# A gated mix of two attentions: f32r halves in row pairs, one stream of slots, masks inside the row maxima, outputs at unit ends, part of A's queries projected late

## The chip, the cores and the metric

The kernel runs on one core of a Trainium2 chip, in one launch. The core has five engines that run side by side and meet only through semaphores: TensorE (PE, matmuls, with its weight loads shown as PEld), VectorE (DVE), ScalarE (ACT), GpSimd (POOL) and SyncE (SP, which here issues most DMAs). Matmuls write to PSUM, eight banks of 512 f32 numbers on each of 128 partitions. The metric is the device time of one execution in microseconds (us).

## The reference

Everything is float32. `x` is 2048 tokens by 512; both attentions read the same `x` and have 32 heads of 16 dimensions.

```python
g = sigmoid((x * gate_w).sum(-1, keepdims=True))
# A: softmax attention over all 2048 keys, no mask
q, k, v = split(x @ A_wqkv)
a = softmax(q k^T * 0.25) v @ A_wo
# B: four segments of 512 tokens; causal inside a segment, and a memory of the earlier segments
p = softmax(q_s k_s^T * 0.25 + causal_mask) v_s
a_mem = (phi(q_s) @ M) / (phi(q_s) @ z + 1e-6);  phi(t) = t + 1 if t > 0 else exp(t)
o = sigmoid(beta) * a_mem + (1 - sigmoid(beta)) * p
M += phi(k_s)^T v_s;  z += sum phi(k_s)
b = o @ B_wo
out = g * a + (1 - g) * b
```

## The kernel before, in words

The source is one long schedule written out by hand: the order in which the Python code calls an engine is the order in that engine's queue, and each engine stops at the first instruction whose semaphores are not ready. No planner reorders anything.

**Projections** (in the block `p0`, L228 to L494). A *slot* is the twelve products of one 128 x 512 tile of q, k or v: four contraction tiles by three terms, since x and the weights are each split into a rounded f32r half and the rest. There are 96 slots: for A, 4 chunks of 512 tokens times (4 tiles of q, 4 of k, 4 of v); then the same for B with its memory (`mem_q`, `mem_den`, `mem_k`). `qk_tile` splits each tile of q and k into three bf16 parts (L294 to L316) and stores them in DRAM scratch, `qd` and `kd`. From slot 51 on, `some_max` puts the first row maxima beside the products.

**Attention.** Work is cut into *units* (side, group of 4 heads, chunk of 512 queries). A has 32 units of 16 steps, one for each block of 128 keys; B has 32 units of 4 steps. All A units come first, in the order group then chunk, then all B units. One step has for each of its 4 heads: a *maximum*, run ahead of the scores by 22 steps (12 in B), in which PE multiplies 128 queries by 512 keys in 96 rows of bf16 parts (L174, L185) and DVE reduces the bank to a row maximum (L176; in B L190 adds the causal mask on the way and writes the bank again); a *score* (L560), in which PE multiplies 128 keys by up to 512 queries with 99 rows, three of which carry the negated maximum, and ACT takes the exponential (L563); and the *values* (L579), in which P of an earlier step is multiplied in f32 with 17 columns of v (16 dimensions and a one for the row sum), the four heads in four column groups of the array, two instructions each. In B, POOL zeroes the masked triangle of P (L565). When a unit's maxima are done, `finish_max` splits them on POOL into three bf16 parts, `transpose_max` turns them on PE, and a DMA writes them as rows 96 to 98 of the q tile (L157). PSUM in this part: 3 banks for maxima, 3 for scores, 1 for values, 1 for the rest.

K of A is loaded once for a group (four chunks, three DMAs each, L125 to L127) and used by its four units; q once for each unit (L116 to L118). Loads are issued on SP five steps ahead of the maxima.

**Outputs.** `oraw` (L583) goes to DRAM, the row sums come back, are inverted on DVE, multiplied by gates, sent out, and read back spread over the heads' rows; the scaled rows are split into f32r halves and multiplied by `wo` (L721). For A the scaling runs an octet of heads over all tokens at a time; the output products run beside the B steps, a segment behind, and the last segment's after the last step.

The names that the change and the prediction touch: `load_q`, `load_k`, `max_parts`, `finish_max`, `transpose_max`, `some_max`, `qk_tile`, `score_parts`, `values`, the functions from `invert_load` to `out_products`, and the loop over `steps` at the end.

Of the kernel before, what the change touches and what calls it, by code (L numbers as in the profile page):

```python
# [12 lines left out]
BF16 = mybir.dt.bfloat16  # L13
# [6 lines left out]
S = 2048  # L20
# [9 lines left out]
MASKED = -1.0e9 / SCALE  # L30

LEAD_A = 22         # steps by which the row maxima run ahead of the scores
LEAD_B = 12
LAG_A = 2           # steps by which P @ V runs behind the scores
LAG_B = 3
LATE_T = 3          # steps from the last maximum of a unit to its transposition
PRE = 5             # steps by which loads run ahead of the maxima
# [3 lines left out]
def gated_mix(ctx, tc, x, xT, wqkv, a_wo, b_wq, b_wk, b_wv, b_wo, beta, gate_w, out):  # L41
# [13 lines left out]
    vdA = [dr.tile([NG, 128, 4, 68], F32, name=f"vdA{c}") for c in range(NCH)]  # L55
# [4 lines left out]
    amd = {c: dr.tile([128, NO, CH], F32, name=f"amd{c}") for c in range(1, NCH)}  # L60
    atd = {c: dr.tile([128, NO, CH], F32, name=f"atd{c}") for c in range(NCH)}
    # 32 rows a head: 16 of P @ V, then the sum of P
    odA = [dr.tile([8, 32, S], F32, name=f"odA{o}") for o in range(NO)]
    odB = [dr.tile([H, 32, CH], F32, name=f"odB{c}") for c in range(NCH)]
    rdA = [dr.tile([8, S], F32, name=f"rdA{o}") for o in range(NO)]
    rdB = [dr.tile([H, CH], F32, name=f"rdB{c}") for c in range(NCH)]
    rdM = {c: dr.tile([H, CH], F32, name=f"rdM{c}") for c in range(1, NCH)}

    # ---------------------------------------------------------------- constants
# [3 lines left out]
    identb = const.tile([128, 128], BF16, name="identb")  # L73
    nc.vector.tensor_copy(identb, identf)
    cmask = const.tile([128, CH], F32, name="cmask")
    nc.gpsimd.memset(cmask, 0.0)
    nc.gpsimd.affine_select(out=cmask, in_=cmask, pattern=[[-1, CH]], base=384, channel_multiplier=1,
                            compare_op=ALU.is_ge, fill=MASKED)
    bmask = const.tile([128, 8, DH], F32, name="bmask")
    nc.gpsimd.memset(bmask, 1.0)  # L80
    nc.gpsimd.affine_select(out=bmask, in_=bmask, pattern=[[-16, 8], [0, DH]], base=0, channel_multiplier=1,
                            compare_op=ALU.is_ge, fill=0.0)
    nc.gpsimd.affine_select(out=bmask, in_=bmask, pattern=[[16, 8], [0, DH]], base=15, channel_multiplier=-1,
                            compare_op=ALU.is_ge, fill=0.0)
    gh = const.tile([128, NO], F32, name="gh")
    ogh = const.tile([128, 1], F32, name="ogh")
    glog = const.tile([128, S // 128], F32, name="glog")
    gA = const.tile([128, 128], F32, name="gA")
    gB = [const.tile([128, 128], F32, name=f"gB{c}") for c in range(NCH)]
    ones = const.tile([24, CH], BF16, name="ones")  # L90
    nc.vector.memset(ones, 1.0)
# [3 lines left out]
    # ---------------------------------------------------------------- pools of the attention  # L95
    qp = ctx.enter_context(tc.tile_pool(name="qp", bufs=6))
    kp = ctx.enter_context(tc.tile_pool(name="kp", bufs=8))
    mp = ctx.enter_context(tc.tile_pool(name="mp", bufs=2))
    sm_ps = ctx.enter_context(tc.tile_pool(name="sm_ps", bufs=3, space=PSUM))

    units = [("A", g, c) for g in range(NG) for c in range(NCH)]
    units += [("B", g, c) for c in range(NCH) for g in range(NG)]
    steps = []          # of the scores
    for u in units:
        for i in range(16 if u[0] == "A" else 4):
            steps.append((u, i))
    nA = NG * NCH * 16

    qt, kt_, ktr = {}, {}, {}

    def load_q(u):
        side, g, c = u
        t = qp.tile([128, 4, CH], BF16, tag="q", name=f"q{side}{g}{c}")
        src = qd[side, g // 2, c]
        hs = slice(4 * (g % 2), 4 * (g % 2) + 4)
        nc.sync.dma_start(t[0:48], src[:, hs])  # L116
        nc.sync.dma_start(t[48:80], src[0:32, hs])
        nc.sync.dma_start(t[80:96], src[0:16, hs])  # L118
        qt[u] = t

    def load_k(side, g, c):
        t = kp.tile([128, 4, CH], BF16, tag="k", name=f"k{side}{g}{c}")
        src = kd[side, g // 2, c]
        hs = slice(4 * (g % 2), 4 * (g % 2) + 4)
        nc.sync.dma_start(t[0:48], src[0:16, hs].unsqueeze(0).broadcast_to([3, DH, 4, CH]))  # L125
        nc.sync.dma_start(t[48:80], src[16:32, hs].unsqueeze(0).broadcast_to([2, DH, 4, CH]))  # L126
        nc.sync.dma_start(t[80:99], src[32:51, hs])  # L127
        kt_[side, g, c] = t

    # ------------------------------------------------ row maxima, queries on partitions  # L130
    pmt = {}
    late = []           # (step of the maxima at which to run, function)

    def finish_max(u):
        pm = pmt.pop(u)
        nm = mp.tile([128, 4, 4], F32, tag="nm", name="nm")
        if u[0] == "A":
            nc.vector.tensor_reduce(nm, pm, axis=AX.X, op=ALU.max, negate=True)  # L138
        else:
            nc.vector.tensor_scalar_mul(nm, pm[:, :, :, 0], -1.0)  # L140
        ms = mp.tile([128, 3, 4, 4], BF16, tag="ms", name="ms")
        r1 = mp.tile([128, 4, 4], F32, tag="r1", name="r1")
        r2 = mp.tile([128, 4, 4], F32, tag="r2", name="r2")
        nc.gpsimd.tensor_copy(ms[:, 0], nm)  # L144
        nc.gpsimd.tensor_sub(r1, nm, ms[:, 0])
        nc.gpsimd.tensor_copy(ms[:, 1], r1)
        nc.gpsimd.tensor_sub(r2, r1, ms[:, 1])
        nc.gpsimd.tensor_copy(ms[:, 2], r2)
        return ms

    def transpose_max(u, ms, pool, tag):
        """From (queries; part, head, block of queries) to three rows of queries."""
        pt = pool.tile([128, CH], F32, tag=tag, name="mt_ps")
        nc.tensor.matmul(pt[:48, :128], ms.rearrange("p a h s -> p (a h s)"), identb, start=True, stop=True)
        mt = mp.tile([48, 128], BF16, tag="mt", name="mt")
        nc.scalar.copy(mt, pt[:48, :128])
        nc.sync.dma_start(qt[u][96:99], mt)  # L157

    def max_parts(m):
        """The four products of step m of the maxima, as functions."""  # L160
        u, i = steps[m]
        side, g, c = u
        if i == 0:
            pmt[u] = mp.tile([128, 4, 4, 4 if side == "A" else 1], F32, tag="pm" + side, name="pm")
        pm = pmt[u]
        q = qt[u]

        share = {}

        def part(j):  # L170
            if side == "A":
                ps = sm_ps.tile([128, CH], F32, tag="sm", name="sm")
                h, s = i // 4, i % 4
                nc.tensor.matmul(ps, q[0:96, h, s * 128:(s + 1) * 128], kt_[side, g, j][0:96, h, :],  # L174
                                 start=True, stop=True)
                nc.vector.tensor_reduce(pm[:, h, s, j:j + 1], ps, axis=AX.X, op=ALU.max)  # L176
                return
            s = 3 - i
            n = (s + 1) * 128
            per = 4 // (s + 1)  # L180
            if j % per == 0:
                share["ps"] = sm_ps.tile([128, CH], F32, tag="sm", name="sm")
            ps = share["ps"]
            n0 = j % per * n
            nc.tensor.matmul(ps[:, n0:n0 + n], q[0:96, j, s * 128:(s + 1) * 128],  # L185
                             kt_[side, g, c][0:96, j, :n], start=True, stop=True)
            if j % per == per - 1:
                for e in range(per):
                    r = ps[:, e * n:(e + 1) * n]
                    nc.vector.tensor_tensor_reduce(r, r, cmask[:, CH - n:], 1.0, -3.0e38, ALU.add, ALU.max,  # L190
                                                   pm[:, j - per + 1 + e, s, 0:1])
        return [lambda j=j: part(j) for j in range(4)]

    def after_max(m):
        u, i = steps[m]
        if i == (15 if u[0] == "A" else 3):
            ms = finish_max(u)
            late.append((m + LATE_T, u, ms))

# [671 lines left out]
```

## Time and profile before

| | |
|---|---|
| three runs | 2480.77, 2482.56, 2490.4 us (median 2482.56) |
| profiled execution, its span | 2486.5 us from first to last instruction; the page gives no other time for it |
| mean granted TensorE clock | 0.938 |
| PE / PEld busy | 2180.2 / 840.2 us |
| DVE busy | 1745.8 us |
| ACT busy | 1470.8 us |
| POOL busy | 294.5 us |
| DMA | 182.96 MB, 74 GB/s over the span |

How to read it: busy time is a union of intervals, and PE's matmuls overlap in a pipeline (each is shown 0.38 us long but they start every 0.22 us), so the distance between starts, not the length, is what a matmul costs. A wait is put down to what ended last before it. "Granted clock" is the share of full speed that the TensorE clock had.

### The profile page before, as it was taken

Reading aid. Unit: us, or ns where it says so; the run is one execution under the profiler, and the core shown is the slowest. Engines: PE = TensorE matmul, PEld = TensorE weight load, DVE = VectorE, ACT = ScalarE, POOL = GpSimd, SP = SyncE. Lnnn points to the kernel's source line nnn. Section 1 sums busy time; section 2 is a strip of 40 time slices with the busy share of each in tenths; the row PEclk is TensorE's granted clock in tenths of the full one; section 3 lists DMA queues with packets and bytes.
Section 4 is the critical chain, followed back from the end, with each engine's and each line's share of the span. In section 5 each row is a group of like instructions: output and inputs, shape, how many; then the busy total and the mean of one; then the engine's idle time right before and its main releaser. Section 6 shows DMA issues by size and latency. Waiting matters only on the chain.

```text
span 2486.5 us, 33483 instructions
## 1 busy us (share of the span) xinstructions
PE 2180.2 (88%) x12033; PEld 840.2 (34%) x12033; DVE 1745.8 (70%) x3506; ACT 1470.8 (59%) x2853; POOL 294.5 (12%) x613
## 2 busy tenths in 40 slices
PE   8958999979979879989897997988999967687878
PEld 6745672222222222222222222222222222233335
DVE  5436668868868768877786886877788556565641
ACT  4433437657757657766675775766677844454543
POOL 3011120112000000000000000000000033232331
PEclk9988999989989989999998998999999988897999
DMA  6554431122110210010111001121001234344442
GB/s 204 191 170 129 147 114 44 68 95 69 56 42 13 63 37 23 20 36 22 47 43 43 12 12 37 32 63 36 22 21 31 74 102 116 121 114 131 116 134 91
DMA packets 98887, 182.96 MB, mean 74 GB/s; under 512 B 13392, under 2 KB 50032, under 8 KB 95904
## 3 DMA queue, kind: packets, MB, share of 16 engines
q1 hardware_dynamic: 97216, 179.41, 23.5%
q0 software_dynamic: 1504, 1.40, 0.3%
q8 instruction: 95, 1.56, 0.3%
q14 instruction: 72, 0.59, 0.1%
HBM read 112.72 MB, written 67.26 MB: 72 GB/s over the span
## 4 chain that ended last, share of the span: by engine, by line
PE 70%; DMA 22%; SPq 4%; DVE 1%; issue 1%; ACT 1%; POOL 1%; DVEq 0%; ACTq 0%; POOLq 0%
PE st L560 20%; PE ops L579 20%; PE sm L174 17%; PE pr L250 7%; DMA qB<-qdB 5%; DMA qA<-qdA 4%; DMA kB<-kdB 3%; PE fin L721 2%; DMA qA<-mt 2%; DMA qdA<-q 2%; PE sm L185 1%; SPq L126 1%; DMA vB<-vdB 1%; SPq L116 1%; SPq L127 1%
## 5 line engine op out<-in xcount | busy, mean ns | idle before, releaser
L563 ACT ACTIVATE p<-st 128x512 f32<-128x512 f32 (+1 forms) x2400 | 1247.8, 597 | 716.2 <-PE st L560 686.0
L176 DVE TENSOR_REDUCE pm<-sm 128x1 f32<-128x512 f32 x2048 | 1279.2, 683 | 383.7 <-PE sm L174 381.6
L174 PE MATMUL sm<-kA,qA 96*128 96x512 bf16 x2048 | 789.9, 386 | 148.7 <-DMA qA<-qdA 148.7
L560 PE MATMUL st<-qA,kA 99*128 99x512 bf16 x2048 | 787.5, 386 | 25.6 <-DMA qA<-mt 22.2
L579 PE MATMUL ops<-p,vA 128*17 128x512 f32 x4096 | 545.6, 605 | 0.0
L560 PEld LDWEIGHTS <-kA 99*128 99x128 bf16 x2048 | 200.5, 98 | 622.9 <-issue 417.4
L190 DVE CUSTOM_DVE_ANT_0 sm<-sm,cmask 128x256 f32<-128x256 f32 (+3 forms) x512 | 248.4, 507 | 183.7 <-PE sm L185 175.1
L174 PEld LDWEIGHTS <-qA 96*128 96x128 bf16 x2048 | 202.3, 99 | 358.6 <-DMA qA<-qdA 151.0
L185 PE MATMUL sm<-kB,qB 96*128 96x256 bf16 (+3 forms) x512 | 162.9, 332 | 100.4 <-DMA qB<-qdB 56.7
L144 POOL CAST ms<-nm 128x16 bf16<-128x16 f32 x64 | 14.1, 221 | 1425.0 <-DVE nm L138 1312.5
L560 PE MATMUL st<-qB,kB 99*128 99x256 bf16 (+3 forms) x512 | 164.1, 334 | 2.0 <-DMA qB<-mt 1.6
L579 PEld LDWEIGHTS ops<-p,vA 128*17 128x17 f32 x4096 | 68.1, 95 | 225.0 <-issue 224.4
L565 POOL TENSOR_SCALAR_AFFINE_SELECT p<-p 128x512 f32<-128x512 f32 x128 | 81.5, 637 | 277.4 <-ACT p L563 277.3
L579 PE MATMUL ops<-p,vB 128*17 128x512 f32 (+3 forms) x1024 | 101.6, 473 | 1.6 <-ACT oraw L583 0.8
L560 PEld LDWEIGHTS <-kB 99*128 99x128 bf16 x512 | 51.9, 102 | 131.0 <-issue 104.4
L185 PEld LDWEIGHTS <-qB 96*128 96x128 bf16 x512 | 53.4, 104 | 122.9 <-DMA qB<-qdB 103.1
L294 ACT CAST q<-pr 128x512 bf16<-128x512 f32 x64 | 37.4, 584 | 84.3 <-DMA qdB<-q 38.6
L190 DVE DVE_READ_ACCUMULATOR2_ANT pm<- 128x1 f32 x512 | 72.1, 141 | 0.0
L250 PE MATMUL pr<-xh,wql 128*128 128x512 f32 x128 | 58.2, 455 | 11.4 <-DVE wql L351 9.1
L301 DVE TENSOR_TENSOR r<-pr,q 128x512 f32<-128x512 f32 x64 | 43.8, 685 | 34.0 <-ACT q L294 32.0
L307 ACT CAST q<-r 128x512 bf16<-128x512 f32 x64 | 39.4, 616 | 35.5 <-DVE r L301 34.3
L315 POOL TENSOR_TENSOR q<-r,q 128x512 bf16<-128x512 f32 x32 | 37.3, 1168 | 168.0 <-ACT q L307 168.0
(140 smaller groups left out, 1497.6 us busy)
## 6 DMA issues: line engine op xcount, KB each, us to landing
odA<-oraw SPq DMA_DIRECT2D x32, 256.0 KB
odB<-oraw SPq DMA_DIRECT2D x32, 256.0 KB
raw<-xT SPq DMA_DIRECT2D x7, 1024.0 KB
qdA<-q SPq DMA_DIRECT2D x48, 128.0 KB
kdA<-q SPq DMA_DIRECT2D x48, 128.0 KB
kA<-kdA SPq DMA_DIRECT2D x32, 192.0 KB
qA<-qdA SPq DMA_DIRECT2D x32, 192.0 KB
qdB<-q SPq DMA_DIRECT2D x48, 128.0 KB
```

Of the source, the lines that this page charges most:

```text
L174: nc.tensor.matmul(ps, q[0:96, h, s * 128:(s + 1) * 128], kt_[side, g, j][0:96, h, :], start=True, stop=True)
L176: nc.vector.tensor_reduce(pm[:, h, s, j:j + 1], ps, axis=AX.X, op=ALU.max)
L185: nc.tensor.matmul(ps[:, n0:n0 + n], q[0:96, j, s * 128:(s + 1) * 128], kt_[side, g, c][0:96, j, :n], start=True, stop=True)
L190: nc.vector.tensor_tensor_reduce(r, r, cmask[:, CH - n:], 1.0, -3.0e38, ALU.add, ALU.max, pm[:, j - per + 1 + e, s, 0:1])
L250: nc.tensor.matmul(ps, l(a, k), r(b, k), start=(n == 0), stop=(n == 11))
L301: nc.vector.tensor_sub(r, ps, q1)
L307: nc.scalar.copy(q2, r)
L560: nc.tensor.matmul(ps[:, h % per, :n], k[0:99, h, b * 128:(b + 1) * 128], q[0:99, h, q0:], start=True, stop=True)
L563: nc.scalar.activation(p[:, h - per + 1:h + 1, :n], ps[:, :, :n], AF.Exp, scale=SCALE)
L565: nc.gpsimd.affine_select(out=p[:, :, 0:128], in_=p[:, :, 0:128], pattern=[[0, 4], [1, 128]], base=0, channel_multiplier=-1, compare_op=AL ...
L579: nc.tensor.matmul(ops[32 * h:32 * h + 17, q0:], v[h], p[:, h, :n], start=(i == 0), stop=(i == last), tile_position=(0, 32 * h))
L721: nc.tensor.matmul(ps, l[:, o], r[:, o], start=(n == 0), stop=(n == 23))
```

## The change

**Scores and maxima.** q and k are stored and loaded as two f32r halves (rounded value and rest, 32 rows of f32) in place of three bf16 parts. A q or k tile is now 128 partitions by 2 heads by 512: heads 0 and 1 of a group lie in partitions 0 to 49, heads 2 and 3 in partitions 64 to 113. A maximum contracts 48 rows, a score 50 (two rows carry the two halves of the negated maximum), and consecutive products alternate between the two halves of the partitions. K is loaded for every unit, and by 128-key-row chunks of four DMAs.

**One stream.** All units, A and B in turn, make one list of 2368 slots; a slot is one score product with its exponential (A 64 a unit, B 10). The maxima run 96 slots ahead; B's maxima are put between the maxima of the following A unit. Each slot issues one score, then one maximum, in opposite halves of the partitions. The values come in bursts after every third slot (sixth, in the last 96 slots), in pieces of 128 columns. PSUM: 4 banks for maxima, 3 for scores, 1 shared by values, output products and late projections.

**Masks.** B's causal mask is an f32 tile in SBUF that is taken into the negated minimum reduction, whose elementwise output goes to SBUF; one bank holds up to two rows of it.

**Outputs.** Each octet (8 heads, one chunk) is inverted, scaled and halved on POOL after its second unit ends, by a power and a correction step; its halves go to DRAM, and the output products of a chunk's 128-token block run at the ends of A's units, half the octets at a time. The last chunk's closing products are kept for the end. The last octet alone runs on DVE.

**Late queries.** A's q for chunks 2 and 3 (8 of 96 slots) is projected inside the stream, at the ends of the first eight A units.

**Projections.** Ten idle products come ahead of the first tile; loads are cut finer; the first 96 maxima run in groups of four from slot 14 of B on (their loads from slot 6); the columns of q, k and the rows of wo are permuted on the host so that DRAM writes are whole rows.

The diff, cut to its core:

```diff
-LEAD_A = 22         # steps by which the row maxima run ahead of the scores
-LEAD_B = 12
+SLOTS = {"A": 64, "B": 10}
+NU = 32
+LEAD = 96
+BURST = 3
+LATER = (2, 3)
+MOST = 3
+NP = 6
+GAP = {"A": 2, "B": 5}
+PRE = 20
+NKA, NKB = 8, 2
...
-                qd[side, o, c] = dr.tile([48, 8, CH], BF16, name=f"qd{side}{o}{c}")
-                kd[side, o, c] = dr.tile([51, 8, CH], BF16, name=f"kd{side}{o}{c}")
+                qd[side, o, c] = dr.tile([32, 8, CH], F32, name=f"qd{side}{o}{c}")
+                kd[side, o, c] = dr.tile([32, 8, CH], F32, name=f"kd{side}{o}{c}")
...
+    units = [unit(side, k) for k in range(NU - 1) for side in "AB"] + [unit("B", NU - 1), unit("A", NU - 1)]
+    slots = [(u, j) for u in units for j in range(SLOTS[u[0]])]
...
+    def load_k(u, kc):
+        side, g, c = u
+        t = kbuf[side][knext[side] % len(kbuf[side])]
+        knext[side] += 1
+        src = kd[side, g // 2, kc]
+        for r in range(2):
+            hs = slice(4 * (g % 2) + 2 * r, 4 * (g % 2) + 2 * r + 2)
+            nc.sync.dma_start(raw(t)[64 * r:64 * r + 32], src[:, hs])
+            nc.sync.dma_start(raw(t)[64 * r + 32:64 * r + 48], src[0:16, hs])
+        kt_[u, kc] = t
+
+    def rows(t, h, n):
+        return t[64 * (h // 2):64 * (h // 2) + n, h % 2]
...
+    def max_product(ps, u, h, s, n0, n, k, k0=0):
+        nc.tensor.matmul(ps[:, n0:n0 + n], rows(qt[u][:, :, s * 128:(s + 1) * 128], h, 48), rows(k[:, :, k0:k0 + n], h, 48),
+                         start=True, stop=True)
...
+        if side == "A":
+            kc, s, h = i // 8, i % 8 // 2, 2 * r + i % 2
+            max_product(ps, u, h, s, 0, CH, kt_[u, kc])
+            nc.vector.tensor_reduce(pm[:, h, s, kc:kc + 1], ps, axis=AX.X, op=ALU.max)
+            flush_rows()
...
+            for h, s, n0, w in mine:
+                rows_left.append(lambda h=h, s=s, n0=n0, w=w: nc.vector.tensor_tensor_reduce(
+                    out=tri["rest"][:, 0:w], in0=ps[:, n0:n0 + w], in1=tri["mask"][:, CH - w:], scale=-1.0, scalar=3.0e38,
+                    op0=ALU.add, op1=ALU.min, accum_out=pm[:, h, s:s + 1]))
...
+    def later_tile(c, o):
...
+        def f(i):
+            k, (a, b) = i // 3, ((1, 0), (0, 1), (0, 0))[i % 3]
+            nc.tensor.matmul(ops, halved["q"][:, k, a, o * 128:(o + 1) * 128], halved["x", c][:, k, b],
+                             start=(i == 0), stop=(i == 11))
...
+    def score_part(n):
...
+        ps = banks[1 + n % BURST] if n in wide and n // BURST % 2 else st_ps.tile([128, CH], F32, tag="st", name="st")
...
+            nc.scalar.activation(p[:, h], ps, AF.Exp, scale=SCALE)
...
+            for h in range(4):
+                nc.tensor.matmul(ops[32 * h:32 * h + 17, q0:q0 + 128 * w], v[:, 17 * h:17 * h + 17], p[:, h, c0:c0 + 128 * w],
+                                 start=(i == 0), stop=done, tile_position=(0, 32 * h))
...
+    def octet(side, o, c, t0, vector=False):
...
+                eng.tensor_tensor(r, rec, minus, op=ALU.pow)
+                eng.tensor_mul(e, rec, r)
+                eng.tensor_scalar(e, e, -1.0, 2.0, op0=ALU.mult, op1=ALU.add)
+                eng.tensor_mul(rec, r, e)
...
+        def scale():
+            eng.tensor_mul(k["v"], k["v"], k["inv"])
...
+                eng.tensor_copy(t[:, bs, 0], v)
+                eng.tensor_sub(t[:, bs, 1], v, t[:, bs, 0].bitcast(F32))
...
+        if n < nS:
+            score_part(n)
+        m = n + LEAD
+        if m < nS:
+            loads(m + PRE)
+            max_part(m, lambda: banks[m % 4])
+        run_todo(m)
+        if n >= nS or n % (2 * BURST if n in wide else BURST) == (2 * BURST if n in wide else BURST) - 1:
+            taken = 0
+            if shared:
+                for _ in range(3):
+                    shared.pop(0)()
+            else:
+                taken = some_values(n, 8 if n >= nS or n in wide else most())
```

More of the change, by code (lines that the diff above doesn't have):

```diff
@@ new lines, in gated_mix @@
+    nS = len(slots)
+    maxs = []
+    for k in range(NU):
+        mine = {u: iter(range(32)) for u in range(2)}
+        bs = [k - 1] if 0 < k < NU - 1 else [k - 1, k] if k else []
+        theirs = {r: [(unit("B", b), (r, i)) for b in bs for i in range(5)] for r in range(2)}
+        start, apart = (33, (3, 3)) if k == 1 else (6, (9, 3)) if k < NU - 1 else (23, (3, 3))
+        at_ = [next(m for m in range(len(maxs) + start, len(maxs) + start + 6) if m % 3 == 0)]
+        while len(at_) < 10 * len(bs):
+            at_.append(at_[-1] + apart[len(at_) % 2])
+        for m in range(len(maxs), len(maxs) + 64 + 10 * len(bs)):
+            r = (m + 1) % 2
+            if m in at_ and bs:
+                maxs.append(theirs[r].pop(0))
+            else:
+                maxs.append((unit("A", k), (r, next(mine[r]))))
+        assert not theirs[0] and not theirs[1]
@@ new lines, in gated_mix, with raw @@
+    last_max = {u: m for m, (u, _) in enumerate(maxs)}
+    a_last = sorted(last_max["A", k % NG, k // NG] for k in range(NU))
+    first_max = {u: m for m, (u, _) in reversed(list(enumerate(maxs)))}
+    assert len(maxs) == nS and all(first[u] + LEAD - last_max[u] > 24 for u in units)
+    qt, kt_ = {}, {}
+    def raw(t):
+        return t[:].bitcast(F32)
+    kbuf = {"A": [kp.tile([128, 2, CH], F32R, name=f"kA{i}") for i in range(NKA)],
+            "B": [kp.tile([128, 2, CH], F32R, name=f"kB{i}") for i in range(NKB)]}
@@ L141, in finish_max @@
[L141 to L198, printed above, removed]
[L200 to L203 removed]
+        ms = mp.tile([128, 2, 2, 2, 4], F32R, tag="ms", name="ms")
+        nv = nm.rearrange("p (r h) s -> p r h s", r=2)
+        nc.gpsimd.tensor_copy(ms[:, :, 0], nv)
@@ new lines, in products, with out_rows, load_block @@
+    def products(ps, t, b, side, o, start, stop):
+        assert (side, o) in ready
+        for i, (x, w) in enumerate(((1, 0), (0, 1), (0, 0))):
+            yield lambda i=i, x=x, w=w: nc.tensor.matmul(ps, t[:, b, x], halved[side][:, o, w], start=start and i == 0,
+                                                         stop=stop and i == 2)
+    def out_rows(c, b):
+        return out[c * CH + b * 128:c * CH + (b + 1) * 128, :]
+    fill = []
+    shared = []
+    blocks = []
+    def load_block(c, b, os):
+        assert all((side, o, c) in scaled for side in "AB" for o in os)
+        t = fr.tile([128, 2, 2, 2, 128], F32R, tag="blk", name="blk", bufs=2)
+        for i, side in enumerate("AB"):
+            nc.sync.dma_start(raw(t)[:, i, 0:len(os)].rearrange("p o h t -> p o (h t)"),
+                              hd[side, c][os[0]:os[-1] + 1, :, b].rearrange("o p h t -> p o (h t)"))
+        blocks.append(t)
+        loaded_blocks[c, b, os] = len(blocks)
@@ new lines, in gated_mix, with output, f @@
+    loaded_blocks = {}
+    def output(c, b, pairs, then, ps=ops):
+        ks = [(os, o, i) for os in pairs for o in os for i in range(2)]
+        for k in ks:
+            def f(n, k=k):
+                os, o, i = k
+                assert loaded_blocks[c, b, os] > len(blocks) - 2
+                t = blocks[loaded_blocks[c, b, os] - 1][:, i, o % 2].unsqueeze(1)
+                list(products(ps, t, 0, "AB"[i], o, k == ks[0], k == ks[-1]))[n]()
+                if k == ks[-1] and n == 2:
+                    then(ps, c, b)
+            for n in range(3):
+                yield lambda n=n, f=f: f(n)
@@ new lines, in gated_mix, with keep, leave @@
+    part = {}
+    def keep(ps, c, b):
+        part[b] = fr.tile([128, D], F32, tag="part", name="part")
+        nc.scalar.copy(part[b], ps)
+    def leave(ps, c, b):
+        t = fr.tile([128, D], F32, tag="res", name="res", bufs=2)
+        from_bank(n)(t, ps)
+        if b in part:
+            nc.gpsimd.tensor_add(t, t, part.pop(b))
+        at(n + 6, lambda: nc.sync.dma_start(out_rows(c, b), t))
+    last = NCH - 1
+    pairs = range(0, 2), range(2, 4)
+    between = {("A", g, c): (c - 1, g // 2, pairs[g % 2:g % 2 + 1], (keep, leave)[g % 2]) for c in range(1, NCH) for g in range(NG)}
@@ new lines, in gated_mix @@
+    for g in (6, 7):
+        del between["A", g, last]
+        at(wide.start - 24, lambda g=g: load_block(last - 1, 3, pairs[g % 2]))
+    fill.extend((wide.start, f) for f in output(last - 1, 3, pairs, leave, banks[0]))
+    for u, (c, b, (os,), _) in between.items():
+        at(end[u] - 20, lambda a=(c, b, os): load_block(*a))
+    for u in units[1:]:
+        at(max(0, first[u] - 30), lambda u=u: load_v(u))
+    for k in range(KT):
+        load_halves("q", "A", wqkv[:, 0:D], (k,), 2 + 16 * k, [10 + 16 * k])
+        load_halves(("x", LATER[0]), "B", x_later(LATER[0]), (k,), 10 + 16 * k, [18 + 16 * k])
@@ L849, in build @@
+    octet("A", NO - 1, last, None, vector=True)
+    assert len(stored) == len(units)
+    del fill[:]
+    for b in range(4):
+        close(0, "A", NO - 1, b)
+        for _, f in fill[-3:]:
+            f()
+        t = fr.tile([128, D], F32, tag="v" if b % 2 else "res", name="res", bufs=2)
+        (nc.scalar.copy if b % 2 else nc.vector.tensor_copy)(t, banks[b])
+        nc.sync.dma_start(out_rows(last, b), t)
 def build():
```

890 lines of the change are left out of this document (465 added, 425 removed).

## The prediction

> **What bounds the kernel now.** First the page's busy times.
>
> ```profile
> span 2486.5 us, 33483 instructions
> PE 2180.2 (88%) x12033; PEld 840.2 (34%) x12033; DVE 1745.8 (70%) x3506; ACT 1470.8 (59%) x2853; POOL 294.5 (12%) x613
> ...
> PE 70%; DMA 22%; SPq 4%; DVE 1%; issue 1%; ACT 1%; POOL 1%; DVEq 0%; ACTq 0%; POOLq 0%
> ```
>
> PE is the busiest and makes 70% of the chain that ended last; DMA waits make 22%. An average over stages says little, so next the busy times by stage: projections up to 162.6 us, a hole, projections with first maxima, A's steps, B's steps, the tail.
>
> ```profile
> 0.00:162.60 162.60, 149.16 (x619) 118.62 (x619) 81.13 (x144) 74.10 (x130) 24.48 (x55) 1.00 0.64 203
> 162.60:197.30 34.70, 0.41 (x4) 0.08 (x2) 0.48 (x1) 0.00 (x0) 5.26 (x8) 0.55 0.30 103
> 197.30:373.40 176.10, 175.82 (x815) 123.98 (x815) 125.22 (x217) 77.80 (x142) 34.97 (x38) 0.99 0.41 130
> 373.40:1985.00 1611.60, 1471.52 (x8179) 430.64 (x8178) 1263.65 (x2137) 1085.43 (x2115) 81.40 (x212) 0.95 0.14 41
> 1985.00:2440.20 455.20, 349.00 (x2263) 140.96 (x2259) 262.95 (x983) 223.34 (x446) 145.22 (x298) 0.87 0.40 118
> 2440.20:2486.50 46.30, 34.28 (x163) 25.89 (x162) 12.39 (x26) 10.14 (x21) 3.16 (x3) 0.93 0.26 94
> ```
>
> The columns after the length are PE, PEld, DVE, ACT and POOL busy, granted clock, DMA share, GB/s. The attention takes 1611.6 + 455.2 = 2066.8 us of 2486.5. One A step from the timeline, first PE, then DVE and ACT beside it:
>
> ```profile
> 1102.29 0.38 PE L174 MATMUL sm<-kA,qA 96*128 96x512 bf16 x1
> 1102.60 1.05 PE L579 MATMUL ops<-p,vA 128*17 128x512 f32 x8
> 1103.58 0.39 PE L560 MATMUL st<-qA,kA 99*128 99x512 bf16 x1
> 1103.81 0.38 PE L174 MATMUL sm<-kA,qA 96*128 96x512 bf16 x1
> ...
> 1105.43 1.05 PE L579 MATMUL ops<-p,vA 128*17 128x512 f32 x8
> ```
>
> ```profile
> 1101.39 2.48 DVE L176 TENSOR_REDUCE pm<-sm 128x1 f32<-128x512 f32 x4 [0.35 <-PE sm L174]
> ```
>
> ```profile
> 1101.17 2.06 ACT L563 ACTIVATE p<-st 128x512 f32<-128x512 f32 x4 [0.77 <-PE st L560]
> ```
>
> A step is 1105.43 - 1102.60 = 2.83 us and PE fills it: values 0.98 (1103.58 - 1102.60), eight products about 0.22 apart, 0.31 from the last product to the values where 0.22 is usual, so 0.09 for the switch. DVE needs 2.48 for its four maxima (0.62 each) and then waits 0.35 for PE; ACT needs 2.06 (0.515 each). So in A, PE is the bound, DVE 12% behind it. 512 such steps are 1449 us; the other 163 of 1611.6 are waits at unit changes and the clock that they lose:
>
> ```profile
> PE sm L174 <- DMA qA<-qdA: 148.7, 8, 34.3
> ```
>
> Eight waits: one is the hole before 197.3, the others stand where a new group's K and q are loaded at once.
>
> **DVE, which the change leaves as it is.** Its maxima by shape:
>
> ```profile
> L176 DVE TENSOR_REDUCE pm<-sm 128x1 f32<-128x512 f32 x2048 | 1279.2, 683 | 383.7 <-PE sm L174 381.6
> ...
> L190 DVE CUSTOM_DVE_ANT_0 sm<-sm,cmask 128x512 f32<-128x512 f32 x128 | 87.4, 707 | 117.2 <-PE sm L185 114.5
> ...
> L190 DVE DVE_READ_ACCUMULATOR2_ANT pm<- 128x1 f32 x512 | 72.1, 141 | 0.0
> L190 DVE CUSTOM_DVE_ANT_0 sm<-sm,cmask 128x384 f32<-128x384 f32 x128 | 69.5, 581 | 22.8 <-PE sm L185 22.5
> ...
> L190 DVE CUSTOM_DVE_ANT_0 sm<-sm,cmask 128x256 f32<-128x256 f32 x128 | 54.0, 437 | 22.9 <-PE sm L185 20.5
> ...
> L190 DVE CUSTOM_DVE_ANT_0 sm<-sm,cmask 128x128 f32<-128x128 f32 x128 | 38.5, 301 | 20.9 <-PE sm L185 17.6
> ...
> L138 DVE TENSOR_REDUCE nm<-pm 128x16 f32<-128x64 f32 x32 | 7.0, 220 | 3.2
> ```
>
> The new stream keeps the 2048 A maxima and the 512 masked ones with their accumulator reads. 96 A maxima run in the projections. The rest is 1952 x 0.62 = 1210, plus 87.4 + 72.1 + 69.5 + 54.0 + 38.5 = 321.5, plus 31 x 0.22 = 7: **1539 us**. The masked ones now write to SBUF instead of over the bank, which no row shows; from below I bound it by the plain reduction's 0.62 in place of 87.4 / 128 = 0.68 (0.06 x 320 bank widths, 20 us less), from above by nothing gained.
>
> **PE in the stream.** What an f32r product costs is in the projections (first two rows), what its weights cost in the third; then values of 384 and 128 columns, each with the row that follows it; last, eight weight loads of the values.
>
> ```profile
> 64.14 0.39 PE L250 MATMUL pr<-xh,wkh 128*128 128x512 f32 x1
> 64.37 0.39 PE L250 MATMUL pr<-xh,wkl 128*128 128x512 f32 x1
> ```
>
> ```profile
> L250 PEld LDWEIGHTS pr<-xh,wkl 128*128 128x128 f32 x64 | 12.0, 188 | 3.5 <-DVE r L301 1.0
> ```
>
> ```profile
> 2064.85 0.84 PE L579 MATMUL ops<-p,vB 128*17 128x384 f32 x8
> 2065.62 0.34 PE L560 MATMUL st<-qB,kB 99*128 99x384 bf16 x1
> ...
> 2068.72 0.41 PE L579 MATMUL ops<-p,vB 128*17 128x128 f32 x8
> 2069.06 0.24 PE L154 MATMUL mt_ps<-identb,ms 128*48 128x128 bf16 x1
> ```
>
> ```profile
> 2422.82 0.13 PEld L579 LDWEIGHTS ops<-p,vB 128*17 128x17 f32 x8 [0.23 <-issue]
> ```
>
> An f32r product of 512 columns starts 0.23 us after the last, like bf16; going from 96 or 99 rows to 48 or 50 saves nothing alone. The gain must come from two products in different halves of the partitions running together, and no row of this trace has that. From below a pair costs 0.23 (full overlap); in between 0.38 (products overlap, but two weight loads of 0.19 come one after the other); from above 0.46 (no overlap). I take 0.23: the values' products do run four at a time in column groups, and their eight loads ended within 0.13 us, so loads to different parts of the array overlap there. The Trainium skill (TensorEngine Tiling, Key Properties) says the same of all tiles, that different ones can load weights and multiply in parallel; by it the pair is 0.23, by the single loads' row 0.38 and the time the second rival's.
>
> The values cost 0.77 for 384 columns and 0.34 for 128, so about 0.56 for 256. Three pieces in a burst are one group of 384 half of the time and 128 + 256 the other: (0.77 + 0.90) / 2 = 0.84, and 0.09 for the switch: 0.93 after every three slots. Three pairs make 0.69. PE thus needs 1.62 a burst where DVE needs 3 x 0.62 = 1.86 in A's slots and more where a B slot (321.5 / 320 = 1.0) is among them. Over 2272 slots that is 1227 us; 24 A units carry 12 output products and 8 carry 12 late ones (32 x 12 x 0.23 = 88), and 64 small transposes, 0.24 each by the L154 row, come to 15: 1330, under DVE's 1539. While PE is in a burst, DVE has up to four banks, 2.48 us of work. So **DVE becomes the bound**, and PE's wait goes to banks that DVE has not yet emptied. ACT has 0.515 a slot (0.62 is DVE's), plus copies; it stays under.
>
> **What is moved.** K loaded by unit is 16 DMAs each time in place of 12 for four units. With q, v, the maxima's rows, `oraw`, octets (5 DMAs each) and output blocks I count about 45 issues on SP for 74 slots (one A and one B unit, 49 us of DVE).
>
> ```profile
> L125 SPq DMA_DIRECT2D kA<-kdA x32: 681/763/3873, 155.6 to 1717.7; - x32
> L126 SPq DMA_DIRECT2D kA<-kdA x32: 616/1352/6288, 156.4 to 1721.1; - x32
> ```
>
> At the minimum of about 0.65 us that is 29 of 49 us, and each key chunk is asked for 20 slots (12 us) ahead. Bytes: about 6 MB in 49 us, 120 GB/s, where the projections moved 203. Hidden, then; but if a semaphore holds SP for more than those 12 us, K is late and PE, DVE and ACT stop in turn. I leave 30 us for such events, a fifth of the 148.7 of today, since the loads no longer come all at once. POOL gets the octets.
>
> ```profile
> L630 POOL TENSOR_TENSOR raw<-raw,inv 128x512 f32<-128x512 f32 x16 | 19.9, 1264 | 74.9 <-DMA qA<-mt 45.3 <-issue 22.6 <-DMA inv<-rdA 7.0
> ```
>
> It had 294.5 us of work; the new longest chain is four such operations, 5 us, and runs between B's units. If it falls on a B unit's masking, which is queued behind it on POOL, the values that need the masked tile wait, and PE with them; that is in the 30.
>
> **Projections.** The first 162.6 us held 51 slots; 8 of them go, 162.6 x 43 / 51 = 137. The hole of 34.7 us arose because K and q were wanted three slots after they were asked for; now there are eight slots between: I take 5, with bounds 0 and 35. The part with maxima, 176, stays: PE fills it, and 96 maxima replace 88. Extra casts go to ACT, busy 44% there (77.80 of 176.10). The idle products warm the clock while the first load is under way; I take 0 to 7, and 2 back. Together 137 + 5 + 176 + 2 = **320**.
>
> **End.** The last 96 slots have no maxima and run at ACT's 0.515 with a little for values: **53**. The tail was 46.3, with four blocks of 24 products; now all but 12 products are done before, and the chain that stays is store, load, invert, store, load, scale and one product group: **22**, from 18 to 30.
>
> Sum: 320 + 1539 + 30 + 53 + 22 = 1964 us against the profiled span of 2486.5, that is 522.5 less (53 from the projections, 445 from the attention, 24 from the tail). The span lies 3.9 above the median of the runs and inside their spread, so I take the difference from the median: **1960 us**.
>
> **Rivals.**
>
> *Weight loads one after the other* (17%): pairs at 0.38. A burst is 1.14 + 0.93 = 2.07, PE 2272 / 3 x 2.07 + 103 = 1671, which passes DVE's 1539. 320 + 1671 + 30 + 75 - 4 = 2092. For it: the 0.19 against 0.23 today. Against it: the eight loads in 0.13.
>
> *The rows don't pair* (8%; the change doesn't do what it says): 0.46 a pair, burst 2.31, stream 1852, total 2273. Still faster, since the waits at unit changes and B's thin stage go.
>
> *The clock* (11%): PE now waits for banks in every burst. In B's stage, where PE waited often, 349.00 of 455.20 busy, the granted clock was 0.87, that is 26% of the time at half. With PE's 1330 doubled in 26% of the stream and DVE's 1539 in the rest: 0.26 x 2660 + 0.74 x 1539 = 1830, total 2251. Against it: B's waits were for DMAs of up to 9 us, the new ones are below 1 us. The Trainium skill (TensorE: Matmul & The Clock Gate, A second HAM failure mode: psum-queue depth-cycling) tells of just this, short waits between groups on PSUM banks letting the clock swing; by that rule the time is this rival's, and the trace cannot decide, since A's PE never waited that way.
>
> *SP's queue, slower than before* (5%): if issues take what they took under pressure (1.35 median, and two to six where the queue was held), 45 of them are 61 us and more in 74 slots. SP becomes the bound above 49 / 45 = 1.1 us each; the kernel is slower from (2486.5 - 395) / 30.7 / 45 = 1.51 us each; at 2 us it is 30.7 x 90 + 395 = 3160. For it: K is issued five times as often (512 DMAs, not 96). Against it: spread loads met 0.65 us.
>
> **Numbers.** The forecast has 59%. It alone lies between 1905 (B's masked maxima cheaper, no stalls, a short start) and 2030 (hole back, twice the stalls). With the second case and the milder half of the clock's, 8 in 10 lie in 1890 to 2150. A measurement of this kernel can tell about 0.5% from no change, 12 us; only SP's case ends above: faster 0.94, same 0.01, slower 0.05.
>
> **What would show it.** Right: DVE over 90% busy in the stream, its maxima 0.62 apart; score and maximum starting nearly together on PE; PE's waits ending on DVE. Second rival: PE never idle, weight loads 0.19 apart. Third: starts 0.23 apart. Clock: half speed in a quarter of the stream. SP: K's landing last ahead of PE's waits. The forecast is wrong as a whole if DVE is busy under 85% of the stream.

## The result and the profile after

The changed kernel takes **1786.7 us** (median of 1785.8 to 1787.3), the kernel before 2486.5 on the same chip; the ratio is 0.718, 95% interval 0.716 to 0.720. The prediction of 1960 was 173 too high, and the time lies below its range. The direction was right, and so was the end of the waits for DMA; the price of DVE's work was too high, and that of PE's too low. Times here and below are medians over all executions of a kernel; the ratios leave out two executions at a lower granted clock, 2315.1 us in the first experiment and 2170.6 us in the one with five products in the fuller half.

Busy times and the chain that ended last, from the page of the changed kernel:

```profile
span 1784.1 us, 40690 instructions
PE 1774.3 (99%) x14945; PEld 913.3 (51%) x14945; DVE 1574.0 (88%) x3330; ACT 1437.8 (81%) x2753; POOL 641.0 (36%) x748
...
PE 94%; DVE 2%; DMA 1%; ACT 1%; POOL 1%; issue 0%; SPq 0%; POOLq 0%; DVEq 0%; ACTq 0%
```

DMA's 22% of the chain is down to 1%, and PE has 94%. Where the time lies is read from the busy times by stage. The stages are: projections without maxima, projections with them, the stream up to the last maximum, the last 96 slots, the tail. After the length come PE, PEld, DVE, ACT and POOL busy, granted clock, DMA share, GB/s:

```profile
0.00:162.60 162.60, 158.28 (x698) 128.85 (x699) 61.20 (x105) 84.42 (x145) 21.11 (x40) 0.99 0.70 230
162.60:308.20 145.60, 144.63 (x675) 100.17 (x673) 108.02 (x204) 66.71 (x115) 38.88 (x39) 1.00 0.57 191
308.20:1708.70 1400.50, 1400.31 (x13111) 646.54 (x13114) 1396.99 (x3007) 1237.49 (x2395) 552.28 (x639) 1.00 0.49 134
1708.70:1761.20 52.50, 52.20 (x386) 23.57 (x379) 3.10 (x6) 47.70 (x98) 28.72 (x30) 1.00 0.39 124
1761.20:1784.10 22.90, 18.87 (x90) 14.13 (x82) 4.67 (x10) 1.50 (x3) 0.00 (x0) 1.00 0.25 82
```

Against the terms of the prediction: projections 308.2 (320), stream 1400.5 (1539 + 30 = 1569), last slots 52.5 (53), tail 22.9 (22). Of the sum's error of 180 us the stream has 168.5 and the projections 12. In the stream PE (1400.31) and DVE (1396.99) are both busy nearly all the time, at full clock; in the kernel before neither was.

DVE's maxima over the whole kernel, by shape (96 of the 2048 plain ones lie ahead of the stream); behind the count come us busy, mean ns of one, and the idle time before:

```profile
L226 DVE TENSOR_REDUCE pm<-sm 128x1 f32<-128x512 f32 x2048 | 1281.0, 683 | 11.8 <-PE sm L205 11.6
...
L238 DVE CUSTOM_DVE_ANT_0 rest<-sm,mask 128x512 f32<-128x512 f32 x128 | 87.6, 684 | 0.0
L238 DVE CUSTOM_DVE_ANT_0 rest<-sm,mask 128x384 f32<-128x384 f32 x128 | 70.1, 548 | 0.0
L238 DVE CUSTOM_DVE_ANT_0 rest<-sm,mask 128x256 f32<-128x256 f32 x128 | 53.1, 415 | 0.0
L238 DVE DVE_READ_ACCUMULATOR2_ANT pm<- 128x1 f32 x512 | 42.8, 84 | 0.0
L238 DVE CUSTOM_DVE_ANT_0 rest<-sm,mask 128x128 f32<-128x128 f32 x128 | 36.6, 286 | 1.9 <-PE sm L205 0.5
```

The plain maxima last as long as before. The masked rows with their reads (READ_ACCUMULATOR, which fetches a row's result) are busy 290.2 us, where the prediction's lines add up to 321.5. What they cost is in the timeline of DVE in the changed kernel (start, us, operation):

```profile
802.98 0.41 DVE L238 CUSTOM_DVE_ANT_0 rest<-sm,mask 128x256 f32<-128x256 f32 x1
803.32 0.08 DVE L238 DVE_READ_ACCUMULATOR2_ANT pm<- 128x1 f32 x1
803.32 0.69 DVE L226 TENSOR_REDUCE pm<-sm 128x1 f32<-128x512 f32 x1
803.92 0.41 DVE L238 CUSTOM_DVE_ANT_0 rest<-sm,mask 128x256 f32<-128x256 f32 x1
...
904.19 4.27 DVE L226 TENSOR_REDUCE pm<-sm 128x1 f32<-128x512 f32 x7
```

Operations overlap. A masked row of 256 keys lasts 0.41, yet 0.34 after its start its accumulator is read *and* the next maximum starts: the read and the end of the row cost nothing. Seven maxima in a row last 4.27: six starts and one whole duration, so they start (4.27 - 0.68) / 6 = 0.598 apart. The same could be seen in DVE's timeline of the kernel before:

```profile
2057.90 0.14 DVE L190 DVE_READ_ACCUMULATOR2_ANT pm<- 128x1 f32 x1
2057.90 0.60 DVE L190 CUSTOM_DVE_ANT_0 sm<-sm,cmask 128x384 f32<-128x384 f32 x1
2058.42 0.14 DVE L190 DVE_READ_ACCUMULATOR2_ANT pm<- 128x1 f32 x1
2058.42 0.60 DVE L190 CUSTOM_DVE_ANT_0 sm<-sm,cmask 128x384 f32<-128x384 f32 x1
```

A row of 384 keys comes 0.52 after the last, where busy times add 0.60 and 0.14. Over the 512 masked rows of the kernel before, the times from a row's start to its read add up to 217 us.

PE's timeline over one burst of three slots:

```profile
799.82 0.60 PE L786 MATMUL ops<-p,vA 128*17 128x256 f32 x6
800.36 0.50 PE L729 MATMUL st<-qA,kA 50*128 50x512 f32 x1
800.36 0.73 PE L205 MATMUL sm<-kA,qA 48*128 48x512 f32 x2
800.70 0.63 PE L729 MATMUL st<-qA,kA 50*128 50x512 f32 x2
800.93 0.40 PE L205 MATMUL sm<-kA,qA 48*128 48x512 f32 x1
801.26 0.63 PE L786 MATMUL ops<-p,vA 128*17 128x256 f32 x8
801.82 0.50 PE L729 MATMUL st<-qA,kA 50*128 50x512 f32 x1
```

Score and maximum start together: three pairs at 800.36, 800.70 (second maximum inside the x2 row) and 800.93. So a pair costs 0.23 as predicted, but the first takes 0.34, and the values begin 0.33 after the last pair: 0.90 from first score to values where the prediction had 0.69 + 0.09 = 0.78. This is a usual burst: over the 502 of this form in the stream the time to the values is 0.906 in the median and 0.886 at the least. Values of 256 columns take 0.56 (801.26 to 801.82), as predicted.

### The profile page after: what moved, and what is told of

It is laid out like the page before. It is cut to its first block, busy times and chain, and to the rows that moved or that the text cites. A ratio compares the mean times of both kernels' runs of the same rounds, so it can differ in the third digit from the quotient of the medians.

```text
span 1784.1 us, 40690 instructions
## 1 busy us (share of the span) xinstructions
PE 1774.3 (99%) x14945; PEld 913.3 (51%) x14945; DVE 1574.0 (88%) x3330; ACT 1437.8 (81%) x2753; POOL 641.0 (36%) x748
## 4 chain that ended last, share of the span: by engine, by line
PE 94%; DVE 2%; DMA 1%; ACT 1%; POOL 1%; issue 0%; SPq 0%; POOLq 0%; DVEq 0%; ACTq 0%
PE ops L786 33%; PE st L729 27%; PE sm L205 14%; PE pr L311 10%; PE ops L898 4%; PE ops L669 2%; PE sm L898 2%; POOL mn L377 1%; DMA raw<-xT 1%; PE num L499 0%; DVE pm L226 0%; DMA qdB<-q 0%; ACT ex L384 0%; DVE q L380 0%; PE mt_ps L196 0%
## 5 line engine op out<-in xcount | busy, mean ns | idle before, releaser
L752 ACT ACTIVATE p<-st 128x512 f32<-128x512 f32 x2261 | 1189.2, 600 | 152.8 <-PE sm L205 100.7
L729 PE MATMUL st<-qA,kA 50*128 50x512 f32 x2014 | 663.1, 432 | 0.0
L205 PE MATMUL sm<-kA,qA 48*128 48x512 f32 x2048 | 658.7, 428 | 0.2
L786 PE MATMUL ops<-p,vA 128*17 128x128 f32 (+3 forms) x6432 | 552.0, 441 | 0.0
L729 PEld LDWEIGHTS st<-qA,kA 50*128 50x128 f32 x2014 | 327.4, 185 | 415.2 <-ACT p L752 371.0
L205 PEld LDWEIGHTS sm<-kA,qA 48*128 48x128 f32 x2048 | 330.4, 185 | 15.6 <-issue 7.1
L848 POOL TENSOR_TENSOR rcp<-rec,minus 128x32 f32<-128x32 f32 x43 | 234.2, 5447 | 75.7 <-DMA rec<-dend 71.0
L238 DVE CUSTOM_DVE_ANT_0 rest<-sm,mask 128x128 f32<-128x128 f32 (+3 forms) x512 | 247.3, 483 | 1.9 <-PE sm L205 0.5
L205 PE MATMUL sm<-kB,qB 48*128 48x128 f32 (+3 forms) x512 | 166.0, 384 | 0.0
L729 PE MATMUL st<-qB,kB 50*128 50x512 f32 (+1 forms) x495 | 109.1, 329 | 0.3 <-ACT mt L199 0.3
```

Of the source, the lines that this page charges most:

```text
L205: nc.tensor.matmul(ps[:, n0:n0 + n], rows(qt[u][:, :, s * 128:(s + 1) * 128], h, 48), rows(k[:, :, k0:k0 + n], h, 48), start=True, stop=True)
L238: rows_left.append(lambda h=h, s=s, n0=n0, w=w: nc.vector.tensor_tensor_reduce(out=tri["rest"][:, 0:w], in0=ps[:, n0:n0 + w], in1=tri["mas ...
L729: nc.tensor.matmul(ps[:, n0:n0 + CH - q0], rows(k[:, :, b * 128:(b + 1) * 128], h, 50), rows(q[:, :, q0:], h, 50), start=True, stop=True)
L752: nc.scalar.activation(p[:, h], ps, AF.Exp, scale=SCALE)
L786: nc.tensor.matmul(ops[32 * h:32 * h + 17, q0:q0 + 128 * w], v[:, 17 * h:17 * h + 17], p[:, h, c0:c0 + 128 * w], start=(i == 0), stop=done ...
L848: eng.tensor_tensor(r, rec, minus, op=ALU.pow)
```

## The experiments

The theory after the result: DVE's work by its starts is 1952 x 0.598 + 209 + 7 = 1383 us (209 being the sum over the 512 masked rows of the time from a row's start to its accumulator's read: 0.61, 0.47, 0.34 and 0.21 by width), and the stream runs at it. The rivals: PE is the bound and DVE only looks full; the masked rows are cheaper because they write to SBUF; the gain is mostly the waits at unit changes and not the pairing. The experiments ran on three chips, where the kernel before took 2485.0 to 2489.4 us; differences in us are against the 1786.7 above, so some 3 us of each mean nothing.

### Masked rows over the bank again

```
-                    out=tri["rest"][:, 0:w], in0=ps[:, n0:n0 + w], in1=tri["mask"][:, CH - w:], scale=-1.0, scalar=3.0e38,
+                    out=ps[:, n0:n0 + w], in0=ps[:, n0:n0 + w], in1=tri["mask"][:, CH - w:], scale=-1.0, scalar=3.0e38,
```

> The changed kernel, but the masked maxima of B write their elementwise output over the bank they read, as before the change, in place of an SBUF tile. In the changed kernel's trace the 512 masked operations start 0.21, 0.34, 0.47 and 0.61 us before their accumulator reads (128 to 512 columns), and the next operation starts with the accumulator read; in the trace of before a further 0.17 us often lay between a read and the next masked operation. Theory 'mis-read price' (the cost was always about 0.41 each and my sum of busy times was wrong): within 6 us of the changed kernel's 1786.7. Rival 'the write to PSUM cost the 0.17': 512 x 0.17 = 87 us more on DVE, about 1870.

Measured 1788.5 us, ratio 0.719 (0.716 to 0.721): 2 us more, which can't be told from none. Where the masked rows are written is not why DVE costs less than predicted.

### Masked rows back to back

```
-            rows_left.pop(0)()
+            flush_rows()
```

> The changed kernel, but the second masked row of a bank is reduced right after the first, with no plain maximum of A between them. Theory 'mis-read price': within 6 us of 1786.7. Rival 'the plain maximum between them hides the accumulator read': 192 of 512 masked operations would follow another one directly and cost 0.17 more, 33 us, about 1820.

Measured 1800.7 us, ratio 0.724 (0.722 to 0.726): 14 us more, between the two expectations. DVE's timeline of this run shows why:

```profile
846.83 0.29 DVE L238 CUSTOM_DVE_ANT_0 rest<-sm,mask 128x128 f32<-128x128 f32 x1
847.05 0.08 DVE L238 DVE_READ_ACCUMULATOR2_ANT pm<- 128x1 f32 x1
847.17 0.56 DVE L238 CUSTOM_DVE_ANT_0 rest<-sm,mask 128x384 f32<-128x384 f32 x1
847.65 0.08 DVE L238 DVE_READ_ACCUMULATOR2_ANT pm<- 128x1 f32 x1
847.65 1.28 DVE L226 TENSOR_REDUCE pm<-sm 128x1 f32<-128x512 f32 x2
```

Ahead of another masked row the read holds DVE for 0.12 (847.05 to 847.17); ahead of a plain maximum for nothing (847.65 twice). 192 reads are followed by a masked row here, 23 us of DVE, of which 14 reached the end. The read as such is not the cost: by the semaphores in the trace, each of these 192 rows waits for the one that the read before it sets. In the kernel before, the 160 masked rows that wait in this way start 0.17 after the read, while 124 of the 299 that wait only for PE's product start together with it, as at 2057.90 above. In both kernels the rows that wait are those that write a tile which the row just before them wrote (there the bank, here `rest`); that this is the reason for the wait was not tested. So putting the second row of a bank after the next plain maximum, as the change does, is worth 14 us.

### DVE relieved

```
-            nc.vector.tensor_reduce(pm[:, h, s, kc:kc + 1], ps, axis=AX.X, op=ALU.max)
+            nc.vector.tensor_reduce(pm[:, h, s, kc:kc + 1], ps[:, 0:256], axis=AX.X, op=ALU.max)
```

> The changed kernel, but each of A's maxima is taken over the first 256 of the 512 keys of its bank only, so the rows are not shifted by their true maximum (this part of the computation is left out); all products, exponentials and values stay. DVE's work in the stream falls from about 1390 to about 880 us. If DVE alone is the bound and PE needs the 1330 us that I predicted: 1786.7 - 70 = about 1717. If PE is the bound beside it (in the trace a burst of three pairs takes 0.90 us and values 0.84 on average, 1.74 x 757 + 103 = about 1421): no gain, 1775 to 1790. If ACT were the bound (1237 us busy): about 1630.

Measured 1777.7 us, ratio 0.714 (0.712 to 0.717): 9 us less. The busy times of its stream:

```profile
309.40:1701.00 1391.60, 1391.60 (x13110) 637.52 (x13112) 937.75 (x3008) 1236.17 (x2395) 551.82 (x639) 1.00 0.49 135
```

DVE loses 459 us of its 1397 and the stream 9: with DVE out of the way PE takes 1391.6. Its bursts go at PE's own pace in both kernels: the time from the first score to the values is 0.905 in the median here and 0.906 in the changed kernel. The prediction's 1330 for PE was 62 too low, and PE stands right beside DVE.

### PE relieved

```
-            for h in range(4):
+            for h in range(4) if side == "B" or done or i // 4 % 2 == 0 else ():
```

> The value products of every second block of 128 keys in A's units are left out (half of the keys do not reach A's output; the sums of P go without them too). PE loses about 975 pieces of 0.21 us in the stream, 205 us; DVE's and ACT's work stays. If PE alone sets the stream: about 1582. If DVE, whose operations by their pitch are 1952 x 0.598 + 209 + 7 = 1383 us, stands right beside it: 1765 to 1782.

Measured 1778.4 us, ratio 0.715 (0.713 to 0.716): 8 us less. So PE alone isn't the bound either:

```profile
308.00:1698.00 1390.00, 1363.13 (x10214) 653.29 (x10213) 1384.46 (x3005) 1220.05 (x2394) 552.45 (x638) 0.99 0.50 135
```

DVE is busy 1384.46 of 1390, against 1383 by its starts: with half of PE's value products out of the way, the stream takes nearly what DVE's starts add up to.

### Both relieved

This kernel has both edits.

> Both cuts at once: every second block's value products left out in A, and A's maxima taken over 256 of the 512 keys (so half of the keys reach neither the maximum nor, by another half, the output). Each cut alone gains 5 to 20 us if PE and DVE stand side by side. Together they should gain far more than the sum: PE about 1392 - 205 = 1187, DVE about 1090, so ACT with 1237 busy becomes the bound: 308 + 1240 to 1275 + 75 = 1623 to 1658. If something else holds the stream (banks handed round, SP, POOL), the time stays above 1740.

Measured 1717.9 us, ratio 0.690 (0.689 to 0.692): 69 us less, where the two cuts alone gave 9 and 8. That is what two bounds side by side do: only when both give way does the time fall. But it isn't the 1623 to 1658 expected with ACT as the next bound:

```profile
306.80:1640.00 1333.20, 1307.50 (x10214) 595.44 (x10213) 960.00 (x3007) 1210.29 (x2394) 552.87 (x640) 1.00 0.51 141
```

ACT is busy 91% and nothing is full. What holds the stream at 1333 stays open. The bursts are uneven in this kernel, since every second block has no values; in the trace ACT sits idle 113.6 us ahead of its exponentials, mostly for PE's products, and PE in its turn pauses some 110 times, 26 us in all, so the two seem to wait for each other by turns. That was not tested.

### Score and maximum in the same half

```
+    def half_of(n):
+        (side, _, _), j = slots[n]
+        return j - 8 if side == "B" and j >= 8 else j % 4 // 2
...
-            r = (m + 1) % 2
+            r = half_of(m - LEAD) if m >= LEAD else m // 2 % 2
             if m in at_ and bs:
-                maxs.append(theirs[r].pop(0))
+                maxs.append((theirs[r] or theirs[1 - r]).pop(0))
             else:
-                maxs.append((unit("A", k), (r, next(mine[r]))))
+                i = next(mine[r], None)
+                if i is None:
+                    r = 1 - r
+                    i = next(mine[r])
+                maxs.append((unit("A", k), (r, i)))
...
-        h = (0, 2, 1, 3)[j % 4]
+        h = j % 4
```

> The changed kernel with the heads in the order 0, 1, 2, 3, and each maximum in the same half of the partitions as the score of its slot, so that three of four neighbours no longer lie in different halves. Same products, same bytes. If pairs run together (in the trace they start 2 to 4 ns apart and the pairs 0.236 us apart): a burst takes 0.47 us more, 757 x 0.47 = 355 more on PE, 2100 to 2160. If pairing is worth nothing: 1787.

Measured 1950.7 us, ratio 0.787 (0.781 to 0.792): 164 us more, not 355. The order of the program offers an explanation. In a burst of three slots the heads' halves now run 001, 100, 110 or 011, so of the six products four are in one half and two in the other, and the two halves still run beside each other. That made a law to test: a burst costs as much as the fuller half has products.

### Five products in the fuller half

```
-            r = (m + 1) % 2
+            r = half_of((m - LEAD) // BURST * BURST) if m >= LEAD else m // 2 % 2
```

The heads' order is that of the changed kernel here, 0, 2, 1, 3, so `half_of` of an A slot is j % 2; the rest of the edit is that of the run above.

> The three maxima of a burst are taken in the partition half that holds most of its three scores. By the plan the fuller half then gets 4.97 products a burst (3.00 in the changed kernel, 4.00 in the run with score and maximum in one half), 757 bursts. Theory, each half works its own list and a burst lasts as long as the fuller list: 1.97 x 757 x 0.226 = 337 us more, less the 10 by which PE trails now, 2105 to 2130. Rival, that the 164 of the earlier run came from the order of the heads and the banks and not from the halves: no more than its 1951, up to 1980.

Measured 2107.0 us, ratio 0.847 (0.845 to 0.849), inside the 2105 to 2130 of the law and far above the rival's 1980. One of its bursts in PE's timeline (the line numbers are 8 higher):

```profile
801.41 0.51 PE L737 MATMUL st<-qA,kA 50*128 50x512 f32 x2
801.75 0.63 PE L213 MATMUL sm<-kA,qA 48*128 48x512 f32 x2
802.22 0.39 PE L737 MATMUL st<-qA,kA 50*128 50x512 f32 x1
802.46 0.39 PE L213 MATMUL sm<-kA,qA 48*128 48x512 f32 x1
802.77 0.84 PE L794 MATMUL ops<-p,vA 128*17 128x128 f32 x16
```

Two scores of different halves start together at 801.41, the second ahead of a maximum that the program has before it: each half works its own list. Of 500 such bursts 491 start in this order. Then come four products of the full half, 0.23 apart; 1.36 to the values, where the changed kernel has 0.90. So 3, 4 and 5 products in the fuller half take 1787, 1951 and 2107 us. One more step of 156 to 164 gives an estimate of 2263 to 2271 for no pairing at all, which was not run. By this estimate the pairing is worth some 480 of the 700 us.

### All of A's queries early

```
-            s0 = now[0] - (4 if c in LATER else 0)
+            s0 = now[0]
...
-            for o in range(NO if c not in LATER else 0):
+            for o in range(NO):
...
-                if side == "A" and c == 0:
-                    shared.extend(later_tile(LATER[g // NO], g % NO))
```

> All of A's queries are projected ahead of the stream again; the loads and splits of the output weights stay late. The eight tiles are 96 products of 0.23 us, 22 us in the projections, and they leave eight places of three products in the stream of PE. If DVE alone sets the stream, nothing comes back there and the time is 1787 + 22 = 1809. If PE stands beside it, the stream gives most of the 22 back: 1779 to 1795.

Measured 1806.1 us, ratio 0.726 (0.724 to 0.728): 19 us more. Its stream, from the later first score on:

```profile
329.60:1727.00 1397.40, 1394.59 (x13167) 646.06 (x13170) 1394.06 (x3007) 1233.60 (x2387) 515.43 (x599) 1.00 0.47 129
```

It begins 21 us later and gets 3 back. The expectation that PE's 22 us would come back was badly argued: where two engines stand side by side, relieving one gives next to nothing, as the run with fewer value products shows too. Work moved from the projections into the stream rode along almost free.

### The kernel before, with earlier loads

```
-        m = min(m, len(steps) - 1)
+        m = min(m + (8 if m < nA - 8 else 0), len(steps) - 1)
```

> The kernel before with one edit: in A's part the loads for the maxima run thirteen steps ahead in place of five. It asks how much of the 700 us lay in the waits at the unit changes alone (PE's eight waits for q, 148.7 us in the profile of before, 34 of them in the hole between 162.6 and 197.3). If those waits are lateness of the request, the seven in the attention, about 115 us, go and the kernel takes 2350 to 2400. If the loads are slow whenever they are issued together, nothing or little comes back: 2450 to 2490.

Measured 2384.4 us against 2485.0, ratio 0.960 (0.958 to 0.963): 101 us less, as expected of late requests. The wait of PE for A's q:

```profile
PE sm L174 <- DMA qA<-qdA: 49.6, 8, 33.3
```

148.7 became 49.6, and 33.3 of that is the hole in the projections, which this edit leaves. So some 100 of the 700 us could have been had without the rest, and the waits are not most of the gain.

### No idle products

```
-        for _ in range(10):
+        for _ in range(0):
```

> The ten idle products at the start of the changed kernel are left out. The prediction put their worth at 0 to 7 us, and at 2. If the granted clock climbs as early without them: 1785 to 1788. If they are what brings the clock up before the first real products (it is full from about 24 us on): 1789 to 1794.

Measured 1786.9 us, ratio 0.719 (0.718 to 0.721): no difference. The clock does not need them: without them it is granted at 1.00 in every stretch of the first 30 us, with them it is at 0.59 and 0.55 from 10 to 14 us and at 1.00 from 14 us on (not from 24).

## Why the prediction was right and wrong

**The step that failed is the price of DVE's work**, "1952 x 0.62 = 1210, plus 87.4 + 72.1 + 69.5 + 54.0 + 38.5 = 321.5". Both numbers take durations where starts count. The 321.5 adds up busy times of operations that overlap; by their starts the rows take 209, and 217 already in the kernel before, so most of these 112 us never existed. The 0.62 divides the 2.48 of four maxima by four, but 2.48 is three starts and one whole duration: 3 x 0.598 + 0.68. That is 0.022 x 1952 = 43 too many. DVE's term was 1383 and not 1539, as the run with fewer value products shows (1390, DVE busy throughout); with the 30 us of stalls that didn't come, less the 17 by which the stream exceeds 1383, this is the whole 168. The same prediction priced PE's products by their starts.

**PE's estimate, 1330, was too low by 62.** The pair at 0.23 was right, and so were the values of 256 columns. A burst's two switches were priced at 0.09 together and cost 0.21 beyond the three pairs: 0.11 at the first pair and 0.10 ahead of the values. This is 0.12 in each of 757 bursts, 91 us; other terms of the 1330 must then have been some 29 too high, and which ones stays open. Under a DVE term of 1539 none of that mattered. With DVE at its true 1383 it makes PE an equal bound, so "DVE becomes the bound" was half of what happened. Of the signs, DVE over 90% busy came (1396.99 of 1400.50), and so did scores and maxima starting together; the maxima lie 0.598 apart and not 0.62. The sign that PE's waits end on DVE did not come. What the trace shows is idle time of the weight loads (PEld) until ACT empties a score bank:

```profile
PEld st L729 <- ACT p L752: 403.5, 781, 0.9
```

PE itself is busy 1400.31 of 1400.50 us meanwhile, so little of it can have held PE up.

**Weight loads one after the other: wrong.** The weight loads of the burst at 800.36 shown above:

```profile
800.35 0.18 PEld L729 LDWEIGHTS st<-qA,kA 50*128 50x128 f32 x1 [0.42 <-issue]
800.36 0.29 PEld L205 LDWEIGHTS sm<-kA,qA 48*128 48x128 f32 x2
800.47 0.44 PEld L729 LDWEIGHTS st<-qA,kA 50*128 50x128 f32 x2
```

In the first two pairs the loads of the two halves start 3 to 4 ns apart and last 0.18 each, so they run side by side. The Trainium skill (TensorEngine Tiling (Array Packing), Key Properties), that different tiles load and multiply in parallel, is borne out. **Rows don't pair: wrong**, though its 2273 is close to the 2263 to 2271 that are estimated above for no pairing.

**The clock: wrong.** It is granted at 1.00 all through the stream. The short waits of PE in every burst, on which this rival rested, did not come: in the trace, where the ends of matmuls are modelled, PE is idle 0.19 us of 1400.50. The Trainium skill's rule (TensorE: Matmul & The Clock Gate, A second HAM failure mode: psum-queue depth-cycling) would have had the clock swing if PE idled between its groups, so the changed kernel is no test of it. In the run with fewer value products PE does idle, 27 us of 1390 in pauses of up to 0.54 us, and the granted clock is 0.99 there.

**SP's queue: wrong.** The issues of the spread K loads, from the groups by line (min/median/max ns):

```profile
L165 SPq DMA_DIRECT2D kA<-kdA x256: 302/370/1912, 140.4 to 1680.6; - x128
```

A median of 0.37 us, where the prediction took 0.65 as the least.

**Projections, last slots and tail** came within 12, 0.5 and 1 us. The hole is gone altogether (5 were left for it) and the late projections are worth 19 us. The idle products, taken at 2, are worth nothing that can be measured. Whether the other steps of these sums were right, or erred in ways that cancel, no run shows.

## What to carry to other kernels

Price a stream of operations on one engine by the time from start to start of neighbours in the timeline, never by the sum of busy times or by a group's length over its count: tails overlap, and the reads of accumulators cost nothing here when the next operation does not wait for them. When a prediction moves the bound to another engine, price the old one as carefully, because the gain ends where the second engine stands, and relieving either alone then gives next to nothing (9 and 8 us here, and 69 together). For products on partial rows, count the products of each half between two switches; the fuller half set the time in the three kernels measured here.

## What the hardware showed that was not expected

- The two halves of the partitions work their own lists: a product of one half starts ahead of an earlier one that waits for its own half (both scores at 801.41 above). Each further product in the fuller half of a burst cost 156 to 164 us in 757 bursts, 0.21 us each.
- A read of DVE's accumulator costs nothing where the next operation does not wait for its semaphore; where it does, the next operation starts 0.12 us after the read (192 rows of the run with masked rows back to back) or 0.17 us after it (160 rows of the kernel before).
- A power on POOL is dear, 5.45 us for 128x32; 43 of them make 234 of POOL's 641 us. From the changed kernel's groups of instructions (us busy, mean ns of one, then the idle time before):

```profile
L848 POOL TENSOR_TENSOR rcp<-rec,minus 128x32 f32<-128x32 f32 x43 | 234.2, 5447 | 75.7 <-DMA rec<-dend 71.0
```

It is hidden here: POOL has 1% of the chain.
